# GpSimd gets xl and the scaling of r one attention slot later, from the seventh 128 tokens on

## The chip, the core and the metric

The kernel runs on one NeuronCore of a Trainium2 chip. TensorE (PE) multiplies matrices, VectorE (DVE), ScalarE (ACT) and GpSimd (POOL) work on tiles, and SyncE (SP) issues all DMAs here. Each engine runs its own instructions strictly in order. The metric is the time of one execution on the device in microseconds (us), the median of several runs.

## The reference

```python
def _attn_ref(r, k, v, w, u):            # (4, 8, 768, 48) each, u (8, 48)
    state = zeros((B, H, D, D))
    for t in range(S):
        cur = einsum('bhd,bhe->bhde', u[None] * kt, vt)
        y[:, :, t] = einsum('bhd,bhde->bhe', rt, state + cur)
        state = wt[:, :, :, None] * state + einsum('bhd,bhe->bhde', kt, vt)

x = y as (3072, 384)
h = x @ w_in;  g = h if h >= 1, 0 if h <= -1, else (h + 1)**2 / 4;  x = g @ w_out     # d_ff 2048
h = x @ w_in2; g = h * sigmoid(1.702 * h);                          out = g @ w_out2   # d_ff 2048
```

A linear attention with a decaying state (RWKV), then two MLPs on its 3072 tokens.

## The kernel before

**The MLPs.** Tokens are cut into eight tiles of 384, the hidden dimension into 16 pieces of 128. One step of the program (`step(s)`) is one piece of one tile: nine matmuls `gemm1` (`hp<-xh,whi`, `hp<-xl,whi`, `hp<-xh,wlo`), the activation, and nine matmuls `gemm2` (`acc<-...`) for the step three before (`LAG = 3`). Each float32 operand is split in a high and a low half to be multiplied in a faster format, so each product is three matmuls: `xh` and `xl` are the halves of the MLP's input, `gh` and `gl` those of the activation, `whi` and `wlo` those of the weights. In the first MLP the activation goes round the engines: VectorE clamps `hp` into `t` (L696), ScalarE squares it (L697), VectorE takes the maximum with `hp` (L709), ScalarE rounds that into `gh` (L690), and `gl = t - gh` (L684) goes to GpSimd in every second step and to VectorE in the others.

**The attention.** It is done in 24 windows of 128 tokens (`window(n)`, n from 0 to 23), six for each batch; three windows make the input of one MLP tile. While the MLP works on tile i, the windows of tile i+1 are woven in. `window` is a Python generator: each `yield` ends an attention slot, and `attn_slot` advances all open windows by one slot, the older first. A tile of 16 steps has 24 slots, so steps have one or two; a new window is opened when the one before has had eight. What a window does, by its slots:

- slot 1: VectorE's scans of the decay w (`pi<-rk`, L433 and L435) give the products `rr` and `pp`; GpSimd forms r*k*u (`rkn`, L436 and L437).
- slot 2: VectorE scales k with `rr` (L441), GpSimd scales r with `pp` (`rk<-rk,pi`, L443, called the scaling of r below).
- slot 3: ScalarE squares `pi` in place for a range check (L456), so after the scaling has read it; VectorE reduces `rkn` to `bb` (L457).
- slot 4: GpSimd's two selects put `bb` on the diagonal of `ra` (`ra<-bb`, L461); ScalarE copies the scaled r into the other half of `ra` (L469).
- slot 6: TensorE transposes k (`tp`, L476) and forms the scores (`sc`, L481); ScalarE copies `tp` to `ktok` (L483); VectorE merges the scores into `ra` under a mask (`ra<-mask,sc`, L486, called the merge below); GpSimd puts the carried state into `lt` (L452).
- slots 8 to 10: TensorE makes the state's update (`kv`, L505) and the output (`yt<-ra,lt`, L511); ScalarE copies it out (`xr`, L530), and six small DMAs move rows of it (L533).
- slot 12: ScalarE rounds `xr` into `xh` (L544), and `xl = xr - xh` (L545) follows, on VectorE for windows 0 to 5 and on GpSimd from window 6 on (`XL_N = 6`).

So slot 12 of window n-1 and slot 4 of window n are the same call, the older window first.

**The order.** The first 16 steps and the attention ahead of them are placed by a scheduler that works with a model of time. All later steps stand under `tc.manual_schedule()`: there each engine's order is the order in which the Python code issues the instructions. Beside this, weights of both MLPs are converted: for the second MLP VectorE takes the bits apart (L648, L650) and GpSimd adds the parts (`wt<-wt,wb`, L204), after which SyncE stores them.

Of the kernel before, what the change touches and what calls it, by code (L numbers as in the profile page):

```python
# [14 lines left out]
ALU = mybir.AluOpType  # L15
# [7 lines left out]
W = 128  # L23
# [38 lines left out]
XL_N = 6  # L62
# [37 lines left out]
def fast_path(st, tc, rkw_t, nat, v_l, w1, w2, u, out, x2_d, w2_d, flag_i, force):  # L100
    nc = tc.nc
# [248 lines left out]
    with ExitStack() as sa:  # L350
# [65 lines left out]
        def window(n):  # L416
            i = n % 2
            b, j = divmod(n, WPB)
# [9 lines left out]
            pp, rr = pi[:, 0:WW], pi[:, WW:2 * WW + 1]  # L428
# [11 lines left out]
            kw = rk[i][:, NP * W:OW].rearrange("p (a b) -> p a b", b=W)  # L440
            nc.vector.tensor_tensor(out=kw, in0=kw, in1=rr[:, 1:].rearrange("p (a b) -> p a b", b=W + 1)[:, :, 1:W + 1], op=ALU.mult)  # L441
            rw = rk[i][:, 0:NP * W].rearrange("p (a b) -> p a b", b=W)
            nc.gpsimd.tensor_tensor(out=rw, in0=rw, in1=pp.rearrange("p (a b) -> p a b", b=W + 1)[:, :, 0:W], op=ALU.mult)  # L443

            def lt_s(hh, c):
                p = slice(64 * hh, 64 * hh + D)
# [5 lines left out]
                    nc.gpsimd.tensor_tensor(out=lt_s(hh, 0), in0=us[p], in1=pcs[p, :, None].to_broadcast([D, NP, D]), op=ALU.mult)  # L452

            yield
            sq = pi.rearrange("p (a b) -> p a b", b=WW + 1)[:, :, 0:WW]
            nc.scalar.activation(out=sq, in_=sq, func=AF.Square, scale=DSC, accum_out=stat[:, n, 0:1])  # L456
            nc.vector.tensor_reduce(bb, nt[:, 0:MC * D].rearrange("p (a d) -> p a d", d=D), axis=AX.X, op=ALU.add)  # L457
            yield
            for hh in range(2):
                p = slice(64 * (1 - hh), 64 * (1 - hh) + 64)  # L460
# [6 lines left out]
            for hh in range(2):  # L467
                p = slice(64 * hh, 64 * hh + 64)
# [9 lines left out]
            for mc in range(MC):  # L478
                for hh in range(2):
                    p = slice(64 * hh, 64 * hh + D)  # L480
# [3 lines left out]
            for hh in range(2):  # L484
                p = slice(64 * (1 - hh), 64 * (1 - hh) + 64)
# [56 lines left out]
                xl[0, ti] = p2.tile([128, KD, TN], F32R, tag="xl", name="xl")  # L542
            o = xh[0, ti][:, :, off:off + W]
            nc.scalar.activation(out=o, in_=xr[:, 0:KD, :], func=AF.Copy)  # L544
            (nc.vector if n < XL_N else nc.gpsimd).tensor_tensor(out=xl[0, ti][:, :, off:off + W], in0=xr[:, 0:KD, :], in1=o.bitcast(F32), op=ALU.subtract)  # L545
            yield

# [7 lines left out]
        def attn_slot():  # L555
            n = started[0]
            if n < (NW if cur[0] >= 0 else MAXW) and n in vn_t and n in nat_t and (not queue or queue[-1][1] >= GAP[0]):
                started[0] += 1
                queue.append([window(n), 0, n, None])
            for e in list(queue):  # L560
                if e[3] == "x" and tile_of[e[2]][0] > cur[0] + 1:
                    continue
                try:
                    e[3] = next(e[0])
                    e[1] += 1
                except StopIteration:
                    queue.remove(e)
# [17 lines left out]
        with ExitStack():  # L585
# [6 lines left out]
            for hh in range(2):  # L592
                p = slice(64 * (1 - hh), 64 * (1 - hh) + 64)
# [280 lines left out]
```

## Time and profile before

| what | value |
|---|---|
| median of 3 runs | 1015.32 us (1013.87 to 1016.21) |
| the profiled execution's own time | 1015.02 us |
| its span, first to last instruction | 1013.3 us |
| mean granted TensorE clock | 0.975 of full speed |
| busy: TensorE, VectorE, ScalarE, GpSimd | 952.9, 567.3, 538.9, 400.0 us |

A busy TensorE is the rule in this kernel; the places that matter are those at which it waits, and what it waits for there. A row of the timeline gives in brackets the idle time of the engine just ahead of the instruction and what ended it.

### The profile page before, as it was taken

To read this page: it belongs to the slowest core of one execution; us is meant where nothing else is said; L and a number is where in the kernel's file an instruction comes from. 1 tells how busy PE (TensorE), PEld (TensorE's weight loads), DVE (VectorE), ACT (ScalarE), POOL (GpSimd) and SP (SyncE) were. 2 spreads that over 40 slices of the span, in tenths; PEclk is the share of its full clock that TensorE was granted. 3 is DMA by queue.
4 is the path that set the end of the run, shared out by engine and by line. 5 is a ranking of instruction groups with operands and counts; after the bars stand their busy time and mean duration, and the time that the engine had idled before them with its cause. 6 is when DMAs were issued, how large, how long until landed. Compare 5 with 4: busy or idle time off the path is not lost.

```text
span 1013.3 us, 18673 instructions
## 1 busy us (share of the span) xinstructions
PE 952.9 (94%) x6976; PEld 911.2 (90%) x6976; DVE 567.3 (56%) x983; ACT 538.9 (53%) x1279; POOL 400.0 (39%) x416
## 2 busy tenths in 40 slices
PE   4756999999999999999999999999999999999997
PEld 2545889899899899998999999999999999999997
DVE  6889966776777777677764753323232323232321
ACT  4666545666666567666554565555555433333332
POOL 5787744545556454565431441111111111111111
PEclk9957999999999999999999999999999999999999
DMA  8886515444545435553303352222222100000000
GB/s 233 206 227 170 138 25 161 131 116 134 151 125 138 138 99 137 137 153 99 92 20 109 105 155 86 86 87 86 86 86 86 41 22 26 22 24 25 24 1 27
DMA packets 52228, 101.73 MB, mean 100 GB/s; under 512 B 8608, under 2 KB 31392, under 8 KB 52128
## 3 DMA queue, kind: packets, MB, share of 16 engines
q1 hardware_dynamic: 52128, 100.45, 34.9%
q8 instruction: 57, 0.93, 0.4%
q14 instruction: 43, 0.35, 0.1%
HBM read 83.51 MB, written 15.73 MB: 98 GB/s over the span
## 4 chain that ended last, share of the span: by engine, by line
PE 62%; DVE 12%; ACT 9%; DMA 8%; issue 5%; SPq 4%; POOL 0%; ACTq 0%; DVEq 0%; POOLq 0%
PE hp L659 29%; PE acc L677 20%; PE acc L668 10%; DMA rk<-rkw_t 4%; SPq L533 3%; DMA xr<-xr 2%; DVE pi L433 2%; ACT gh L690 2%; DVE t L709 2%; DVE ra L486 2%; DVE pi L435 1%; ACT ra L469 1%; PE yt L511 1%; ACT t L697 1%; DMA wst<-w 1%
## 5 line engine op out<-in xcount | busy, mean ns | idle before, releaser
L684 POOL TENSOR_TENSOR gl<-t,gh 128x384 fp32r<-128x384 f32 x128 | 134.1, 1048 | 441.7 <-ACT gh L690 433.5
L690 ACT ACTIVATE gh<-t 128x384 fp32r<-128x384 f32 x256 | 133.9, 523 | 182.2 <-DVE t L709 77.7
L720 DVE TENSOR_TENSOR t<-t,hp 128x384 f32<-128x384 f32 x128 | 70.8, 553 | 218.6 <-ACT t L715 218.2
L715 ACT ACTIVATE t<-hp 128x384 f32<-128x384 f32 x128 | 62.9, 491 | 145.9 <-PE hp L659 145.8
L668 PE MATMUL acc<-gh,whi 128*128 128x384 f32 x384 | 132.8, 353 | 0.9 <-ACT ev L263 0.6
L668 PE MATMUL acc<-gl,whi 128*128 128x384 f32 x384 | 131.3, 342 | 2.3 <-DVE gl L684 2.3
L668 PE MATMUL acc<-gh,wlo 128*128 128x384 f32 x384 | 130.3, 339 | 0.0
L677 PE MATMUL acc<-wlo,gh 128*128 128x384 f32 x384 | 130.2, 339 | 0.0
L677 PE MATMUL acc<-whi,gh 128*128 128x384 f32 x384 | 129.9, 338 | 0.0
L677 PE MATMUL acc<-whi,gl 128*128 128x384 f32 x384 | 129.4, 337 | 0.0
L684 DVE TENSOR_TENSOR gl<-t,gh 128x384 fp32r<-128x384 f32 x128 | 78.3, 612 | 57.9 <-ACT gh L690 56.0
L697 ACT ACTIVATE t<-t 128x384 f32<-128x384 f32 x128 | 66.4, 519 | 68.5 <-DVE t L696 64.9
L709 DVE TENSOR_TENSOR t<-t,hp 128x384 f32<-128x384 f32 x128 | 70.1, 548 | 54.3 <-ACT t L697 52.8
L659 PE MATMUL hp<-xh,whi 128*128 128x384 f32 x384 | 92.0, 348 | 3.4 <-DVE t L709 3.3
L659 PE MATMUL hp<-xl,whi 128*128 128x384 f32 x384 | 89.4, 341 | 5.0 <-DVE xl L545 5.0
L696 DVE TENSOR_SCALAR t<-hp 128x384 f32<-128x384 f32 x128 | 70.4, 550 | 39.6 <-PE hp L659 39.4
L659 PE MATMUL hp<-xh,wlo 128*128 128x384 f32 x384 | 89.1, 341 | 0.0
L659 PE MATMUL hp<-x2l,whi 128*128 128x384 f32 x384 | 88.8, 339 | 0.0
L659 PE MATMUL hp<-x2h,wlo 128*128 128x384 f32 x384 | 88.0, 337 | 0.0
L659 PE MATMUL hp<-x2h,whi 128*128 128x384 f32 x384 | 87.4, 335 | 0.0
L668 PEld LDWEIGHTS acc<-gh,whi 128*128 128x128 f32 x384 | 72.4, 190 | 6.3 <-ACT ev L263 1.9
L668 PEld LDWEIGHTS acc<-gl,whi 128*128 128x128 f32 x384 | 72.9, 190 | 2.8 <-DVE gl L684 2.4
(107 smaller groups left out, 1865.4 us busy)
## 6 DMA issues: line engine op xcount, KB each, us to landing
wst<-w SPq DMA_DIRECT2D x96, 384.0 KB, 3.4
rk<-rkw_t SPq DMA_DIRECT2D x48, 288.9 KB, 4.9
rkn<-nat SPq DMA_DIRECT2D x24, 384.0 KB, 4.5
lt<-v_l SPq DMA_DIRECT2D x48, 128.0 KB, 3.8
w_d<-wt SPq DMA_DIRECT2D x32, 192.0 KB, 2.7
w2f<-w_d SPq DMA_DIRECT2D x32, 192.0 KB, 2.6
vn<-nat SPq DMA_DIRECT2D x24, 192.0 KB, 3.6
x_d<-ev SPq DMA_DIRECT2D x24, 192.0 KB, 2.2
```

The source lines that it names most:

```text
L433: nc.vector.tensor_tensor_scan(out=rr[:, WW:0:-1], data0=ws[:, WW:0:-1], data1=one_s[:, WW:0:-1], initial=0.0, op0=ALU.mult, op1=ALU.max)
L533: nc.sync.dma_start(out=xr[64 * hh + D:64 * hh + 64, q, :], in_=xr[64 * hh + 16 * q:64 * hh + 16 * q + 16, 3, :])
L659: nc.tensor.matmul(out=hp[:, 0:n], lhsT=win(a, f, kk), rhs=b[:, kk, 0:n], start=(i == 0), stop=(i == 3 * KD - 1))
L668: nc.tensor.matmul(out=acc[j][:, 0:n], lhsT=wout(a, f, j * 128, 128), rhs=b[:, 0:n], start=(f == 0 and i == 0), stop=(f == KF - 1 and i == 2))
L677: nc.tensor.matmul(out=o[:, 0:DM], lhsT=a[:, j * 128:(j + 1) * 128], rhs=wout(b, f, 0, DM), start=(f == 0 and i == 0), stop=(f == KF - 1 a ...
L684: eng.tensor_tensor(out=gl[:, 0:n], in0=t[:, 0:n], in1=gh[:, 0:n].bitcast(F32), op=ALU.subtract)
L690: nc.scalar.activation(out=gh[:, 0:n], in_=t[:, 0:n], func=AF.Copy)
L696: nc.vector.tensor_scalar(t[:, 0:n], hp[:, 0:n], scalar1=-1.0, scalar2=1.0, op0=ALU.max, op1=ALU.min)
L697: nc.scalar.activation(out=t[:, 0:n], in_=t[:, 0:n], func=AF.Square, bias=0.5, scale=0.5)
L709: nc.vector.tensor_tensor(out=t[:, 0:n], in0=t[:, 0:n], in1=hp[:, 0:n], op=ALU.max)
L715: nc.scalar.activation(out=t[:, 0:n], in_=hp[:, 0:n], func=AF.Sigmoid, scale=1.702)
L720: nc.vector.tensor_tensor(out=t[:, 0:n], in0=t[:, 0:n], in1=hp[:, 0:n], op=ALU.mult)
```

## The change

Two instructions of GpSimd are issued later, for the windows from n = 6 on. The scaling of r moves from the end of slot 2 to the start of slot 3, ahead of ScalarE's square of `pi`, which must come behind it. `xl` moves from slot 12 to a slot 13 of its own. Since slot 13 of window n-1 falls in the same call as slot 5 of window n, the selects of window n (slot 4) are now issued ahead of `xl` of window n-1. Nothing is added or removed, and no other engine's order changes in the part that is ordered by hand.

```diff
             rw = rk[i][:, 0:NP * W].rearrange("p (a b) -> p a b", b=W)
-            nc.gpsimd.tensor_tensor(out=rw, in0=rw, in1=pp.rearrange("p (a b) -> p a b", b=W + 1)[:, :, 0:W], op=ALU.mult)
+            if n < XL_N:
+                nc.gpsimd.tensor_tensor(out=rw, in0=rw, in1=pp.rearrange("p (a b) -> p a b", b=W + 1)[:, :, 0:W], op=ALU.mult)
...
             yield
+            if n >= XL_N:
+                nc.gpsimd.tensor_tensor(out=rw, in0=rw, in1=pp.rearrange("p (a b) -> p a b", b=W + 1)[:, :, 0:W], op=ALU.mult)
             sq = pi.rearrange("p (a b) -> p a b", b=WW + 1)[:, :, 0:WW]
             nc.scalar.activation(out=sq, in_=sq, func=AF.Square, scale=DSC, accum_out=stat[:, n, 0:1])
...
             nc.scalar.activation(out=o, in_=xr[:, 0:KD, :], func=AF.Copy)
+            if n >= XL_N:
+                yield
             (nc.vector if n < XL_N else nc.gpsimd).tensor_tensor(out=xl[0, ti][:, :, off:off + W], in0=xr[:, 0:KD, :], in1=o.bitcast(F32), op=ALU.subtract)
             yield
```

Since 24 slots fall on 16 steps, the neighbours of the moved instructions differ from window to window, with a period of three. GpSimd's queue of three windows that follow one another shows all three kinds. (The line numbers behind the change are a few higher: L545 becomes L550, L443 becomes L457, L461 becomes L464, L452 becomes L453, L684 becomes L689. `ra_3644` and so on are the buffers of one window's `ra`; L204 is the add for a weight piece.)

The first kind, here window 14, before:

```order
L443 TENSOR_TENSOR rk_163<-rk_163,pi 128x512
L684 TENSOR_TENSOR gl<-t,gh 128x384
L545 TENSOR_TENSOR xl<-xr,xh 128x3x128
L461 AFFINE_SELECT ra_3644<-bb 64x512
L461 AFFINE_SELECT ra_3645<-bb 64x512
L204 TENSOR_TENSOR wt<-wt,wb 128x384
L452 TENSOR_TENSOR lt_165<-us,pcs 48x4x48 x2
L684 TENSOR_TENSOR gl<-t,gh 128x384
```

and of the change:

```order
L457 TENSOR_TENSOR rk_163<-rk_163,pi 128x512
L689 TENSOR_TENSOR gl<-t,gh 128x384
L464 AFFINE_SELECT ra_3644<-bb 64x512
L464 AFFINE_SELECT ra_3645<-bb 64x512
L204 TENSOR_TENSOR wt<-wt,wb 128x384
L550 TENSOR_TENSOR xl<-xr,xh 128x3x128
L453 TENSOR_TENSOR lt_165<-us,pcs 48x4x48 x2
L689 TENSOR_TENSOR gl<-t,gh 128x384
```

The two selects and the add of a weight piece, which stood behind `xl`, now stand ahead of it.

The second kind, here window 15, before:

```order
L443 TENSOR_TENSOR rk_164<-rk_164,pi 128x512
L204 TENSOR_TENSOR wt<-wt,wb 128x384
L545 TENSOR_TENSOR xl<-xr,xh 128x3x128
L461 AFFINE_SELECT ra_3934<-bb 64x512
L461 AFFINE_SELECT ra_3935<-bb 64x512
L684 TENSOR_TENSOR gl<-t,gh 128x384
L204 TENSOR_TENSOR wt<-wt,wb 128x384
L452 TENSOR_TENSOR lt_166<-us,pcs 48x4x48 x2
```

and of the change:

```order
L204 TENSOR_TENSOR wt<-wt,wb 128x384
L457 TENSOR_TENSOR rk_164<-rk_164,pi 128x512
L464 AFFINE_SELECT ra_3934<-bb 64x512
L464 AFFINE_SELECT ra_3935<-bb 64x512
L689 TENSOR_TENSOR gl<-t,gh 128x384
L550 TENSOR_TENSOR xl<-xr,xh 128x3x128
L204 TENSOR_TENSOR wt<-wt,wb 128x384
L453 TENSOR_TENSOR lt_166<-us,pcs 48x4x48 x2
```

Here the selects and a `gl` moved ahead of `xl`, and the first add moved ahead of the scaling of r.

The third kind, here window 13, before:

```order
L443 TENSOR_TENSOR rk_164<-rk_164,pi 128x512
L684 TENSOR_TENSOR gl<-t,gh 128x384
L545 TENSOR_TENSOR xl<-xr,xh 128x3x128
L461 AFFINE_SELECT ra_3377<-bb 64x512
L461 AFFINE_SELECT ra_3378<-bb 64x512
L684 TENSOR_TENSOR gl<-t,gh 128x384
```

and of the change:

```order
L689 TENSOR_TENSOR gl<-t,gh 128x384
L457 TENSOR_TENSOR rk_164<-rk_164,pi 128x512
L464 AFFINE_SELECT ra_3377<-bb 64x512
L464 AFFINE_SELECT ra_3378<-bb 64x512
L550 TENSOR_TENSOR xl<-xr,xh 128x3x128
L689 TENSOR_TENSOR gl<-t,gh 128x384
```

A `gl` now stands ahead of the scaling of r, and the selects stand ahead of `xl`.

## Rows read from the trace of the kernel before

**Rows 1.** The page, part 2: TensorE's busy tenths in 40 slices of the span.

```profile
PE   4756999999999999999999999999999999999997
```

**Rows 2.** Waits of TensorE from 160 to 545 us: total us, times, longest.

```profile
PE kv L505 <- DVE ra L486: 5.3, 5, 2.1
PE yt L511 <- DVE ra L486: 4.0, 4, 1.7
PE kv L505 <- ACT ktok L483: 0.7, 1, 0.7
PE acc L668 <- ACT ev L263: 0.6, 3, 0.2
```

**Rows 3.** Waits of GpSimd and of VectorE from 160 to 545 us.

```profile
POOL xl L545 <- ACT xh L544: 75.1, 17, 6.8
POOL rk L443 <- DVE pi L435: 44.0, 16, 5.2
...
DVE ra L486 <- POOL ra L461: 13.5, 5, 2.8
```

**Rows 4.** VectorE's timeline, window 10 (third kind): start us, us, instruction, [idle before].

```profile
232.07 1.52 DVE L486 COPY_PREDICATED ra<-mask,sc 64x512 f32<-64x512 int32 x2 [2.83 <-POOL ra L461]
```

**Rows 5.** Timeline at window 11 (first kind).

```profile
251.51 1.01 POOL L545 TENSOR_TENSOR xl<-xr,xh 128x384 fp32r<-128x384 f32 x1 [3.51 <-DVE t L696]
...
252.60 1.67 POOL L461 TENSOR_SCALAR_AFFINE_SELECT ra<-bb 64x512 f32<-64x512 f32 x2
...
253.19 0.56 DVE L684 TENSOR_TENSOR gl<-t,gh 128x384 fp32r<-128x384 f32 x1 [1.70 <-ACT gh L690]
...
254.13 1.34 DVE L648 TENSOR_SCALAR wt<-wst 128x384 int32<-128x384 int32 x1
254.24 1.01 POOL L204 TENSOR_TENSOR wt<-wt,wb 128x384 int32<-128x384 int32 x1
...
256.28 1.50 DVE L486 COPY_PREDICATED ra<-mask,sc 64x512 f32<-64x512 int32 x2
...
256.37 0.58 ACT L483 ACTIVATE ktok<-tp 128x512 f32<-128x512 f32 x1
...
258.04 0.56 PE L505 MATMUL kv<-vn,ktok 64*48 64x48 f32 x16 [1.08 <-DVE ra L486]
```

**Rows 6.** Timeline at window 15 (second kind).

```profile
336.02 0.35 DVE L648 TENSOR_SCALAR wt<-wst 128x384 int32<-128x384 int32 x1
...
339.14 1.00 POOL L545 TENSOR_TENSOR xl<-xr,xh 128x384 fp32r<-128x384 f32 x1 [4.69 <-ACT xh L544]
...
340.81 0.55 DVE L709 TENSOR_TENSOR t<-t,hp 128x384 f32<-128x384 f32 x1 [3.37 <-ACT t L697]
...
342.01 1.95 DVE L684 TENSOR_TENSOR gl<-t,gh 128x384 fp32r<-128x384 f32 x1 [0.18 <-ACT gh L690]
...
342.54 0.99 POOL L204 TENSOR_TENSOR wt<-wt,wb 128x384 int32<-128x384 int32 x1
...
343.50 1.39 POOL L452 TENSOR_TENSOR lt<-us,pcs 48x192 f32<-48x192 f32 x2
...
345.72 0.78 PE L511 MATMUL yt<-ra,lt 128*64 128x64 f32 x16 [1.51 <-DVE ra L486]
```

**Rows 7.** TensorE's timeline at windows 8 (first kind) and 21 (second kind).

```profile
191.06 1.16 PE L505 MATMUL kv<-vn,ktok 64*48 64x48 f32 x30 [2.11 <-DVE ra L486]
...
475.55 1.06 PE L505 MATMUL kv<-vn,ktok 64*48 64x48 f32 x32 [0.72 <-ACT ktok L483]
478.33 1.20 PE L511 MATMUL yt<-ra,lt 128*64 128x64 f32 x16 [1.72 <-DVE ra L486]
```

**Rows 8.** Stretches: us, busy by engine, granted TensorE clock, DMA share, GB/s.

```profile
191.00:196.00 5.00, 4.95 (x59) 4.80 (x60) 3.64 (x9) 3.12 (x9) 2.63 (x3) 0.66 0.49 145
343.00:350.00 7.00, 5.49 (x70) 5.12 (x69) 4.97 (x10) 3.78 (x11) 5.16 (x7) 1.00 0.47 165
475.00:483.00 8.00, 5.72 (x62) 5.46 (x63) 5.91 (x10) 4.27 (x13) 6.16 (x8) 0.79 0.15 51
```

## The prediction

> **What bounds the kernel now.** I read the page's slices first. TensorE's busy share [rows 1] is low in the first four slices, about 100 us, in which the attention is started and weights are converted, and is 9 tenths from there to the end. So outside the start the kernel is bound by TensorE, and time can be won there only where TensorE waits or where its clock is lowered. The attention ends soon after 520 us, so the change has to work between about 160 us, where the first `xl` on GpSimd stands, and there. The list of TensorE's waits of that part [rows 2] is short and complete: 10.6 us in 13 waits, of which 9.3 us in nine waits end with VectorE's merge of the scores into `ra` (L486). They come at two of the three kinds of windows: at `kv` in the first kind (windows 8, 11, 14, 17, 20: 2.11, 1.08 and, from the sum of 5.3, three of 0.7), at `yt` in the second (windows 15 and 21: 1.51 and 1.72; windows 12 and 18 share the remaining 0.8) [rows 2, 5 to 7]. The third kind has none. Two places have a lower clock: 0.66 over the 5 us after 191, 0.79 over the 8 us from 475 [rows 8]. A mean below 1 in a stretch is time at 1.2 instead of 2.4 GHz. The wait of 1.51 at window 15 left the clock at 1.00 [rows 8], so in these rows the clock fell behind 2.11 us, and behind 0.72 and 1.72 us in close order, and not behind 1.51.
>
> Then I asked why the merge is late, in the timelines of both kinds. The obvious link is not the one that costs. VectorE does sit idle for GpSimd's selects ahead of the merge, 13.5 us in five waits [rows 3], but these five are the windows of the third kind, as window 10 [rows 4], at which TensorE does not wait. In the other two kinds VectorE has no idle time ahead of the merge: it is busy, and it is slow. At window 11 its L648 takes 1.34 us beside GpSimd's add L204, against 0.35 elsewhere [rows 5, 6]. At window 15 its `gl` takes 1.95 us beside GpSimd's L204 and the work ahead of it, against 0.56 [rows 5, 6]. So GpSimd's burst behind `xl` falls on the VectorE instructions just ahead of the merge. The burst starts there because GpSimd stands waiting for `xh` with everything else behind it, 75.1 us in 17 waits [rows 3].
>
> **The change, part by part.** *The scaling of r.* GpSimd idles ahead of it in all 16 windows of this part, until the scan L435 has written `pp` [rows 3]. Its start is thus set by the scan and not by its place in the queue, and I cost the later place at nothing for the scaling itself. In the first kind nothing passes it. In the second kind an add L204 (0.99 us) goes ahead into that idle time. In the third a `gl` goes ahead; if its `gh` comes late, the scaling starts up to 1.0 us later. ScalarE's square of `pi` waits behind the scaling, and the next `gh` and `t` queue behind that. What hides it: in 160 to 545 us TensorE never waits for `gh`, `gl` or a free `hp` [rows 2], although VectorE's L709 stood idle 3.37 us for a late `t` at window 15 [rows 6]. So the chain from `hp` to `gl` may be over 3 us late without cost; beyond that each further microsecond would be one of TensorE's.
>
> *The selects ahead of `xl`.* They need `bb`, which is there early, so they and the L204 behind them run in what was GpSimd's idle time before `xl`. `xl` itself starts when `xh` is there, as before; it has its reader in the next tile. What remains behind `xl` is shorter: at window 11, `lt` alone instead of selects, L204 and `lt`.
>
> First kind, from rows 5. Without L204 beside it L648 would take 0.35, so the merge comes 0.99 us earlier. `ktok`, which `kv` needs too, ends at 256.95, 1.09 us ahead of `kv`, and TensorE is free 1.08 ahead, so both allow it. Upper end: 0.99 at windows 8 and 11 and all 0.7 at the other three, 4.1 us. Against it: `xl` ends at 252.52 and `lt` (up to 1.39 us [rows 6]) then runs to 253.91 at most, right where VectorE's `gl` starts at 253.19. If that is held for 0.72 us, the merge and `ktok` are late by it, and 0.3 is left at each: 1.5 us. I take 2.8, the middle, since the rows put `lt` on the start of `gl` but do not say which is first.
>
> Second kind, from rows 6. `xl` 339.14 to 340.14, L204 to 341.13, `lt` to 342.52 at most, while `gl` is ready at 342.01. It is held for 0.51 at most instead of 1.39 (1.95 less 0.56). So the merge comes 0.9 to 1.39 earlier, at windows 15 and 21: 1.8 to 2.8 us, I take 2.4. Windows 12 and 18 I leave as they are.
>
> A rule of the Trainium skill bears on this: "SBUF — State Buffer", section "Who interferes with whom", says that a VectorE instruction with two inputs in SBUF contends with a GpSimd instruction that reads SBUF, and that the later one is blocked in full until the other is done. By it alone `gl` at window 15 would have waited for one GpSimd instruction; the trace shows it behind two in a row, through L204's end at 343.53 [rows 6], so I take the rows. The rule also speaks against the change, which puts the selects beside VectorE's L648 and L650 of the earlier steps; that is the third rival.
>
> *The clock.* 5 us at 0.66 lose 5 x 0.34 = 1.7 us, 8 us at 0.79 lose 8 x 0.21 = 1.7 [rows 8]. With the terms above the wait at window 8 shrinks from 2.11 to about 1.5 and that of window 21 from 1.72 to about 0.5. Both are then no longer than the 1.51 that left the clock alone, so I count both back: 3.4 us, with 0 as the other end.
>
> *The start.* Window 7's scaling leaves the part that the scheduler places, and a few neighbours swap there. TensorE's slices there are full already [rows 1]; I cost it at nothing, with 1 us to either side.
>
> Sum: 2.8 + 2.4 + 3.4 = 8.6 us off the profiled execution's 1015.0, which is 1006.4. The median of the runs stands 0.3 above that execution, so 1006.7 us. All upper ends (4.1 + 2.8 + 3.4 + 1) give 1004.0, all lower ends (1.5 + 1.8 + 0 - 1) 1013.0.
>
> **The rivals.** *The clock stays low.* The waits shrink as above but at one or both places the clock still falls. For it: the window 8 estimate of 1.5 us is at the edge. Gain 5.2 to 6.9, time 1008.4 to 1010.1, down to 1012 with the small ends of the first two terms.
>
> *Nothing changes.* The change removes what its form suggests, the waits for `xh` and for the selects, and these are idle time beside a busy TensorE: all of VectorE's 13.5 us lie at windows where TensorE doesn't wait. If VectorE's slow instructions are then hit by another GpSimd instruction (`lt`, or a `gl`) for as long, the merge stays where it is: 1015.3, give or take 1.5. Against it: less is left in GpSimd's queue behind `xl`.
>
> *The collisions move to a worse place.* The selects (1.67 us the pair) now run when VectorE works without a pause after the scans, and may stretch its L648 by 0.99 in each of 15 windows. VectorE's cover is the 3.37 us of idle time ahead of L709. It decides from the point at which the stretched chain is more than that late: then the merge is late in the first and second kinds, ten windows, by 1 us each, and with one more fall of the clock (1.7) the kernel ends at about 1015.3 + 10 - 5.2 + 1.7 = 1022 if nothing of the clock comes back; with half of the windows hit it is 1016.8, within the bound below. Against it: one collision of 0.99 is well inside 3.37.
>
> **How the numbers follow.** Chances: forecast 0.57 (own range 1004 to 1008.4), low clock 0.25, nothing 0.11, moved collisions 0.07. The range 1003.5 to 1012.5 takes in the first two with their bounds. Within 0.2%, about what a measurement of this kernel can tell from no change, is 1013.3 to 1017.3. So faster 0.82, same 0.11, slower 0.07.
>
> **What would show it.** In the profile after: GpSimd's wait ahead of `xl` remains but the selects stand ahead of it; VectorE's 13.5 us for selects are gone; L648 takes 0.35 and `gl` under 1.1 ahead of the merge at windows 11 and 15; TensorE's 9.3 us for the merge fall to about 4; the clock stays at 1.00 after 191 and 475. I am wrong if TensorE's waits for the merge are as long as before, if ScalarE waits for the scaling of r by more than a microsecond a window and TensorE for `gh` behind it, or if VectorE's time for L648 and L650 grows and L709 has no idle time left.

## The result and the profile after

The changed kernel takes 1003.62 us (median of 4 runs, 1002.71 to 1004.84). The kernel before, run beside it, took 1015.77 (4 runs, 1013.87 to 1018.0). The ratio is 0.989, 95% interval 0.9878 to 0.9902: 12.2 us faster by the medians (11.2 by the ratio), against 8.6 predicted. The profiled execution took 1002.71 us with a span of 1001.0, which is 12.3 less than before.

First TensorE's list of waits after the change, 160 to 545 us, which answers to [rows 2], and then rows of the same view for its weight loads, for ScalarE, VectorE and GpSimd (those three from 160 to 530 us). The columns are microseconds in total, times, and the longest.

```profile
PE yt L514 <- DVE ra L489: 1.4, 4, 0.4
PE kv L508 <- ACT ktok L486: 1.3, 2, 0.7
PE acc L673 <- ACT ev L263: 0.3, 1, 0.3
...
PEld acc L673 <- ACT ev L263: 2.3, 5, 0.6
...
ACT xh L547 <- DMA xr<-xr: 9.4, 10, 1.3
ACT pi L459 <- POOL rk L457: 3.9, 5, 0.8
...
DVE ra L489 <- PE sc L484: 1.6, 5, 0.3
...
POOL rk L457 <- DVE pi L435: 21.8, 11, 2.7
POOL xl L550 <- ACT xh L547: 19.7, 14, 2.4
...
POOL ra L464 <- DVE bb L460: 13.8, 5, 2.8
```

TensorE's 10.6 us are now 3.0, and none of `kv`'s waits ends with the merge any more. VectorE's 13.5 us for the selects [rows 3] are gone. Two waits are new that bear on the prediction: ScalarE's square of `pi` waits for the scaling of r, 3.9 us in five waits, and GpSimd's selects wait for `bb` at the five windows of the second kind, 13.8 us. These waits are from one execution. In a second profile of the same kernel (e11 below) TensorE's wait for `ktok` is 3.1 us instead of 1.3, and the other waits at `kv` and `yt` are within 0.2.

The timeline of windows 11 and 15 after the change, VectorE, GpSimd and the matmuls that waited, against [rows 5] and [rows 6]:

```profile
247.41 1.00 POOL L550 TENSOR_TENSOR xl<-xr,xh 128x384 fp32r<-128x384 f32 x1 [0.80 <-ACT xh L547]
248.37 1.08 POOL L453 TENSOR_TENSOR lt<-us,pcs 48x192 f32<-48x192 f32 x2
249.09 0.78 DVE L689 TENSOR_TENSOR gl<-t,gh 128x384 fp32r<-128x384 f32 x1 [1.43 <-ACT gh L695]
...
250.25 0.35 DVE L653 TENSOR_SCALAR wt<-wst 128x384 int32<-128x384 int32 x1
250.63 0.56 DVE L655 SCALAR_TENSOR_TENSOR wt<-wst,wt 128x384 int32<-128x384 int32 x1
...
251.23 1.52 DVE L489 COPY_PREDICATED ra<-mask,sc 64x512 f32<-64x512 int32 x2
...
253.38 0.56 PE L508 MATMUL kv<-vn,ktok 64*48 64x48 f32 x16
...
334.20 1.01 POOL L204 TENSOR_TENSOR wt<-wt,wb 128x384 int32<-128x384 int32 x1
...
335.17 1.08 POOL L453 TENSOR_TENSOR lt<-us,pcs 48x192 f32<-48x192 f32 x2
...
336.12 0.56 DVE L689 TENSOR_TENSOR gl<-t,gh 128x384 fp32r<-128x384 f32 x1 [0.18 <-ACT gh L695]
336.71 1.50 DVE L489 COPY_PREDICATED ra<-mask,sc 64x512 f32<-64x512 int32 x2
...
338.46 0.72 PE L514 MATMUL yt<-ra,lt 128*64 128x64 f32 x15
```

At window 11 L653 (the former L648) takes 0.35 instead of 1.34 us, `lt` stretches `gl` by 0.22, and `kv` starts without a wait. At window 15 `gl` takes 0.56 instead of 1.95, and `yt` starts without a wait. The stretches behind windows 8 and 21, where the clock was 0.66 and 0.79 [rows 8] (busy time and instructions of TensorE, its weight loads, VectorE, ScalarE and GpSimd; then the granted clock, the DMA share and GB/s):

```profile
189.00:194.00 5.00, 5.00 (x72) 4.63 (x74) 3.63 (x10) 3.35 (x9) 2.20 (x3) 1.00 0.51 146
466.00:474.00 8.00, 7.63 (x93) 7.10 (x94) 5.76 (x14) 4.73 (x13) 4.03 (x4) 1.00 0.30 72
```

Outside the windows little moved: window 7's `kv` starts at 166.6 us (167.3 before), and from window 23's `kv` to the end it takes 490.9 us (491.0). Between them it takes 343.5 us instead of 355.0, so 11.5 of the 12.3 lie there. Three parts make it up: the 7.6 us of waits (10.6 less 3.0), the two falls of the clock, which the prediction had priced at 3.4, and a wait that the prediction overlooked and that stands in the list of the weight loads before, not in that of the matmuls:

```profile
PEld acc L668 <- ACT ev L263: 1.9, 4, 0.6
...
PEld acc L668 <- DVE ev L261: 1.4, 4, 0.4
```

At the end of an MLP tile VectorE copies one accumulator out (`ev`, L261). In the third kind of windows this copy stood behind the late merge, and TensorE's next `acc` waited 0.35 us for it, four times. After the change that row is gone. With its 1.4 us the three make 12.4, which is 0.9 too much. Matching TensorE's matmuls of both timelines one by one gives less for two of them: 1.5 us at each fall of the clock, so 3.0, and 0.27 to 0.32 us at each of the four windows with `ev`, so 1.2 where the weight loads waited 1.4. The sum is then 11.8, against 11.5.

### The profile page after: what moved, and what is told of

Read it like the earlier page. It is cut to its first block, busy times and chain, and to the rows that moved or that the text cites. A ratio compares the mean times of both kernels' runs of the same rounds, so it can differ in the third digit from the quotient of the medians.

```text
span 1001.0 us, 18691 instructions
## 1 busy us (share of the span) xinstructions
PE 945.8 (94%) x6976; PEld 906.6 (91%) x6976; DVE 562.0 (56%) x983; ACT 538.2 (54%) x1279; POOL 393.4 (39%) x416
## 4 chain that ended last, share of the span: by engine, by line
PE 63%; DVE 13%; ACT 10%; DMA 5%; issue 5%; SPq 3%; POOL 0%; ACTq 0%; DVEq 0%
PE hp L664 29%; PE acc L682 20%; PE acc L673 10%; SPq L536 3%; DVE pi L433 2%; DMA rk<-rkw_t 2%; DMA xr<-xr 2%; ACT gh L695 2%; DVE t L714 2%; ACT ra L472 2%; DVE ra L489 2%; ACT t L702 2%; DVE pi L435 1%; PE kv L508 1%; PE yt L514 1%
## 5 line engine op out<-in xcount | busy, mean ns | idle before, releaser
L689 POOL TENSOR_TENSOR gl<-t,gh 128x384 fp32r<-128x384 f32 x128 | 132.5, 1035 | 497.0 <-ACT gh L695 465.5
L689 DVE TENSOR_TENSOR gl<-t,gh 128x384 fp32r<-128x384 f32 x128 | 75.4, 589 | 63.5 <-ACT gh L695 62.8
L714 DVE TENSOR_TENSOR t<-t,hp 128x384 f32<-128x384 f32 x128 | 70.2, 548 | 54.0 <-ACT t L702 52.5
```

Of the source, the lines that this page charges most:

```text
L689: eng.tensor_tensor(out=gl[:, 0:n], in0=t[:, 0:n], in1=gh[:, 0:n].bitcast(F32), op=ALU.subtract)
L714: nc.vector.tensor_tensor(out=t[:, 0:n], in0=t[:, 0:n], in1=hp[:, 0:n], op=ALU.max)
```

## Experiments

**Theory A:** what cost was GpSimd's burst behind `xl`, which fell on VectorE's last instructions ahead of the merge. With the selects ahead of `xl` it is shorter and earlier. **Rival B:** the later scaling of r carries the gain. **Rival C:** the selects came late for the merge. Each kernel was timed in five rounds; ratios are to the kernel before.

**e1, e2: the two halves of the change alone.** e1 has only this, e2 only the two other places of the diff:

```diff
             nc.scalar.activation(out=o, in_=xr[:, 0:KD, :], func=AF.Copy)
+            if n >= XL_N:
+                yield
             (nc.vector if n < XL_N else nc.gpsimd).tensor_tensor(out=xl...
```

> Only xl one slot later; the scaling of r stays where it was. Theory A (the burst of GpSimd's instructions that stood behind xl fell on VectorE's last instructions ahead of the merge; the selects, the adds L204 and gl now run ahead of xl, so the burst is shorter): nearly the whole gain of 12.2 us, 1003 to 1005.5 us, L648 at window 11 at 0.35 us and gl of VectorE at window 15 under 1.1 us. Rival B (the later scaling of r carries a good part): 1008 us or more. Rival C (what cost was that the selects came late for VectorE's merge): also the whole gain here.

> Only the scaling of r one slot later; xl and all behind it as before. Theory A: nothing of the burst behind xl changes, 1015.8 us, give or take 1.5, and TensorE's waits for the merge stay at 9.3 us. Rival B: 1004 to 1010 us. Rival C: 1015.8 us as A.

e1: 1002.29 us, 0.987 (0.985 to 0.9891). e2: 1017.35 us, 1.0013 (1.0 to 1.0026). The whole gain is in the place of `xl`; B falls. The scaling's move, alone, is no gain and perhaps a small loss (its profile has a third fall of the clock, at window 15).

**e3, e5, e6: `xl` later for one kind of window at a time.** In e3 (whose label is a slip: it is the first kind) the remainder is 1, in e5 2, in e6 0:

```diff
+            if n >= XL_N and n % 3 == 1:
+                yield
             (nc.vector if n < XL_N else nc.gpsimd).tensor_tensor(out=xl...
```

> xl one slot later only where the window that is then at slot 4 or 5 is of the first kind (8, 11, 14, 17, 20); the scaling of r as before. Theory A: the waits for the merge at kv (5.3 us) go and the clock behind window 8 comes back (1.5 to 1.7 us), the waits at yt (4.0 us) stay: 1008 to 1010.5 us. Rival C: VectorE's waits for the selects are at windows of the third kind, which this leaves as they were, 13.5 us in all: 1014 to 1016 us.

> xl one slot later only where the window then at slot 4 or 5 is of the second kind (9, 12, 15, 18, 21); the scaling of r as before. Theory A (shorter burst behind xl): the 4.0 us of waits at yt fall to about 0.7, the clock behind 476 comes back (1.5 us), the 5.3 us at kv and the clock behind window 8 stay: 1015 - 3.3 - 1.5 = 1010.2 us, 1009 to 1012. Rival C (late selects cost): VectorE's 13.5 us of waits for them are at the third kind, which stays: 1014 to 1016 us.

> xl one slot later only where the window then at slot 4 or 5 is of the third kind (10, 13, 16, 19, 22), where VectorE's merge waited 13.5 us for the selects; the scaling of r as before. Theory A: the 13.5 us go and TensorE hardly notices; from the shifts between the two first traces about 1.2 us in all: 1013 to 1015.5 us. Rival C: most of the gain is here, 1009 us or less.

First kind: 1009.63 us, 0.9946 (0.9927 to 0.9965), 5.5 us off. Second: 1009.45 us, 0.9934 (0.9921 to 0.9947), 6.7 off. Third: 1013.4 us, 0.9971 (0.9961 to 0.9981), 2.9 off. C, by which nearly all should lie in the third kind, falls as the main cause; but the third kind is worth more than the 0 of the prediction. The weight loads' waits show why. Those of e3, then of e6:

```profile
PEld acc L670 <- ACT ev L263: 1.3, 3, 0.5
PEld acc L670 <- DVE ev L261: 1.3, 4, 0.4
```

```profile
PEld acc L670 <- ACT ev L263: 1.3, 3, 0.5
```

The wait for `ev` stays where the third kind is as before, and goes in e6. The three gains add to 15.1 us. What they compare with is e1, which moves `xl` alone, with 13.2; the difference is within the intervals. Some may be counted twice: e6's profile also halves the waits at `kv` of windows 14, 17 and 20 (about 0.70 to 0.36, 0.44 and 0.39), which e3 wins too; and e5's has no fall of the clock behind window 8, although its wait there stayed at 2.01 us.

**e4: is it the add L204?** The kernel before, with L204 issued ahead of the first slot of its step, so ahead of `xl` in the first kind:

```diff
+            if l == 0 and i >= 1:
+                add_w2()
             if slots:
...
-                add_w2()
                 if f in PRE_F and nconv[1] < NPC:
```

> The kernel before, with GpSimd's add L204 issued ahead of the first attention slot of its step instead of behind it: in the first kind it then stands ahead of xl, while xl, the selects and the scaling of r stay as before; in the second kind the L204 behind xl keeps its place. Theory A, in the form that it is L204 that held L648: L648 at 0.35 us at windows 8, 11, 14, 17 and 20, most of the 5.3 us of waits at kv gone and the clock behind window 8 back: 1009 to 1012 us, with the 4.0 us at yt left. In the form that any instruction of GpSimd in that place costs the same: lt takes the place of L204, half of that gain, 1012 to 1014 us. Rival C (late selects): the selects are no earlier, 1015.8 us, give or take 1.5.

1011.52 us, 0.9963 (0.9948 to 0.9979). Its timeline at window 11 and, in the last two rows, at window 9 (here L649 and L651 are the former L648 and L650):

```profile
251.89 1.66 POOL L462 TENSOR_SCALAR_AFFINE_SELECT ra<-bb 64x512 f32<-64x512 f32 x2
252.47 0.56 DVE L685 TENSOR_TENSOR gl<-t,gh 128x384 fp32r<-128x384 f32 x1 [1.28 <-ACT gh L691]
...
253.41 0.36 DVE L649 TENSOR_SCALAR wt<-wst 128x384 int32<-128x384 int32 x1
253.52 1.39 POOL L453 TENSOR_TENSOR lt<-us,pcs 48x192 f32<-48x192 f32 x2
253.81 0.74 DVE L651 SCALAR_TENSOR_TENSOR wt<-wst,wt 128x384 int32<-128x384 int32 x1
...
256.77 0.43 PE L506 MATMUL kv<-vn,ktok 64*48 64x48 f32 x10
...
208.83 1.94 DVE L685 TENSOR_TENSOR gl<-t,gh 128x384 fp32r<-128x384 f32 x1 [0.18 <-ACT gh L691]
212.53 0.85 PE L512 MATMUL yt<-ra,lt 128*64 128x64 f32 x16 [1.73 <-DVE ra L487]
```

`xl` and the selects stand where they stood, `lt` has taken L204's place, and L649 takes 0.36: it was L204 that held it, and `kv` no longer waits. All of TensorE's waits for the merge at `kv` are gone from the list (2.4 us for `ktok` are left there); those at `yt` rose from 4.0 to 5.7 us. The rise is at window 9: 0.08 us of wait before, 1.73 here, with a fall of the clock behind it (1.41 in e3, with a fall too). VectorE's `gl` ahead of that merge takes 1.94 us, as in the kernel before (1.96), where TensorE came late enough not to wait for it. So part of the first kind's gain is given back one window later unless the second kind is mended too.

**e7: only the selects moved**, from slot 4 to the end of slot 3; `xl` and the scaling of r keep their slots, so L204 stays behind `xl`. The loop is cut from its place for n from 6 on:

```diff
             nc.vector.tensor_reduce(bb, nt[:, 0:MC * D]...
+            if n >= XL_N:
+                for hh in range(2):
+                    p = slice(64 * (1 - hh), 64 * (1 - hh) + 64)
+                    nc.gpsimd.affine_select(out=ra[hh][p]...
             yield
```

> The kernel before, with only the two selects issued one slot earlier, so that they stand ahead of xl; L204 of the first kind stays behind xl, and xl and the scaling of r keep their slots. Theory A: what stands behind xl is shorter by the selects in all kinds, so L204 runs beside gl or earlier instead of beside L648 and is over before the merge: 1004 to 1008 us. If it is L204's place behind xl as such that costs, whenever it runs: 1013 to 1015 us.

1003.44 us, 0.9877 (0.9862 to 0.9893): the gain of the whole change without moving either of its two instructions. Its timeline at window 11:

```profile
249.27 1.00 POOL L550 TENSOR_TENSOR xl<-xr,xh 128x384 fp32r<-128x384 f32 x1 [1.43 <-ACT xh L549]
250.23 1.01 POOL L204 TENSOR_TENSOR wt<-wt,wb 128x384 int32<-128x384 int32 x1
250.95 0.71 DVE L689 TENSOR_TENSOR gl<-t,gh 128x384 fp32r<-128x384 f32 x1 [1.73 <-ACT gh L695]
251.21 1.55 POOL L452 TENSOR_TENSOR lt<-us,pcs 48x192 f32<-48x192 f32 x2
...
252.05 0.35 DVE L653 TENSOR_SCALAR wt<-wst 128x384 int32<-128x384 int32 x1
```

Without the selects ahead of it L204 is nearly over when `gl` comes, and costs it 0.15 us.

**e8: the changed kernel with the selects behind `xl` again** (the same lines, at the start of slot 5):

```diff
                 nc.scalar.activation(out=ra[hh][p], in_=rt[p], func=AF.Copy)
             yield
+            if n >= XL_N:
+                for hh in range(2):
+                    p = slice(64 * (1 - hh), 64 * (1 - hh) + 64)
+                    nc.gpsimd.affine_select(out=ra[hh][p]...
             if n + 1 < NW:
```

> The changed kernel with the selects one slot later too, so behind xl again as before; in the first kind L204 stands ahead of xl, in the second and third kind the order behind xl is xl, selects, then L204 or gl. Theory A: first kind as with the add issued ahead (its waits at kv mostly gone), second kind as before (waits at yt 4 to 5.5 us, one or two falls of the clock): 1009.5 to 1012 us. If any instruction of GpSimd at that place cost VectorE as much, or the late selects themselves: 1014 to 1016 us.

1008.64 us, 0.993 (0.9917 to 0.9943), a little under the range: some 4 us (by the ratios) to 5 us (by the medians) of the gain are lost with the selects' place alone. VectorE's 13.5 us for them are back as 12.5, the wait for `ev` as 1.7, and at window 15:

```profile
337.63 1.02 POOL L204 TENSOR_TENSOR wt<-wt,wb 128x384 int32<-128x384 int32 x1
338.08 0.99 DVE L694 TENSOR_TENSOR gl<-t,gh 128x384 fp32r<-128x384 f32 x1 [0.19 <-ACT gh L700]
338.61 1.40 POOL L453 TENSOR_TENSOR lt<-us,pcs 48x192 f32<-48x192 f32 x2
```

GpSimd's `gl` has gone ahead of `xl` here, VectorE's `gl` is held by L204 alone, and takes 0.99 instead of 1.95.

**e9 to e12: is there more?** e9 is the changed kernel with `xh` in the later slot too. e10 is e7 with e1's edit as well. e11 is the changed kernel again. e12 is the kernel before with e9's edit, so with the scaling of r in its old slot:

```diff
             o = xh[0, ti][:, :, off:off + W]
+            if n >= XL_N:
+                yield
             nc.scalar.activation(out=o, in_=xr[:, 0:KD, :], func=AF.Copy)
-            if n >= XL_N:
-                yield
             (nc.vector if n < XL_N else nc.gpsimd).tensor_tensor(out=xl...
```

> The changed kernel with ScalarE's xh one slot later too, so that ScalarE does the copies of ra ahead of it and no longer holds them for the DMAs of xr (9.4 us in ten waits in the changed kernel). Theory A: what is left of TensorE's waits in the changed kernel is 1.3 us at kv for ktok, which stands late in ScalarE's queue, and 1.4 us at yt; the first goes, the second stays: 1001.5 to 1003 us against 1003.6. If xh and with it xl come so late that lt behind xl runs beside the merge's last predecessors again: 1005 us or more.

> The selects one slot earlier and xl one slot later, the scaling of r as before: both ways to get the selects ahead of xl at once. Theory A: each alone takes the same waits away, so both together give no more than one: 1002 to 1004 us. If the two gained by different waits, the gains add: below 1000 us.

> The changed kernel itself, for a comparison on the same chip with the two others: 1003.6 us, give or take 1. If the later scaling of r costs something (the kernel with only xl later had 1002.3 us): about 1 us above the others.

> xh and xl one slot later, the scaling of r in its slot of the kernel before. If the later scaling costs a little (the changed kernel lay 1 to 2 us above the two with the scaling as before): 998.5 to 1000 us. Theory A without that: the scaling does nothing either way, 1000.3 us, give or take 1.

e9: 1000.27 us, 0.9852 (0.9838 to 0.9866). e10: 1002.52 us, 0.9875 (0.9859 to 0.9891). e11: 1004.18 us, 0.9895 (0.988 to 0.991). e12: 998.28 us, 0.9829 (0.9813 to 0.9845), the fastest. e10 gives no more than e7, so the two ways win the same waits. Waits of TensorE and, as the third row, of ScalarE in e9; then TensorE's whole list in e12:

```profile
PE yt L514 <- DVE ra L489: 2.2, 5, 0.5
PE kv L508 <- ACT ktok L486: 1.3, 3, 0.8
...
ACT pi L459 <- POOL rk L457: 3.8, 5, 0.8
```

```profile
PE yt L511 <- DVE ra L486: 0.6, 2, 0.3
```

With the scaling in its old slot ScalarE's wait for it is gone and TensorE's 3.5 us of waits are 0.6. The intervals of e9 and e12 just overlap, and those of e1 (0.985 to 0.9891), the changed kernel and e11 do so widely. So a loss of about 2 us by the later scaling between e9 and e12, and of 1.3 to 1.9 between e1 and the changed kernel, is likely and not settled.

## Why the prediction was right, step by step

The mechanism held, but by the medians the gain of 12.2 us was more than all upper ends together, 11.3 (4.1 + 2.8 + 3.4 + 1). The measured 1003.62 us lies outside the forecast's own range of 1004 to 1008.4, and within the stated range by 0.12 us only. That it is within is partly luck: the first kind's term was too small, the third kind's was at nothing, and the clock came back in full for a reason that did not hold.

- **The cause** (GpSimd's burst behind `xl`, not the wait for the selects itself): right. e4 shows L204 holding L648, and e7 and e8 show that the selects' place ahead of or behind `xl` decides how late the burst is. "They need `bb`, which is there early" was wrong at the second kind: there the selects now wait up to 2.8 us for `bb`, which still leaves them ahead of `xl`.
- **First kind, 2.8 us (1.5 to 4.1): too small.** TensorE's waits there fell from 5.3 to 0.7, by 4.6, more than the upper end of 4.1 (to 1.2 in e11, by 4.1). The step that was off is "If that is held for 0.72 us": `lt` stretched `gl` by 0.22 at window 11, and L650, which took 0.74 there before (the row below), takes 0.56 now. Window 8 gained 1.4, more than L648's 0.99; there ScalarE's wait for the DMAs of `xr` was also shorter (1.53 to 0.89 us), which nothing here isolates.

```profile
255.50 0.74 DVE L650 SCALAR_TENSOR_TENSOR wt<-wst,wt 128x384 int32<-128x384 int32 x1
```

- **Second kind, 2.4 us (1.8 to 2.8): right in sum.** `yt`'s waits fell from 4.0 to 1.4, by 2.6. At windows 15 and 21 1.51 and 1.36 went, 2.9 in all and so a little over the upper end; window 9 waits 0.3 more than before. Windows 9, 12, 18 and 21 have 0.36 each.
- **The clock, 3.4 us: about right (3.0 in TensorE's matmuls), the reason too simple.** Both stretches are at 1.00. But that the clock falls behind a longer wait and not behind a shorter one does not hold (last section): in e5 and e6 it stays at window 8 with the wait nearly as it was. So that both falls are gone may in part be chance.
- **Third kind, nothing: wrong, 1.2 to 1.4 us.** "TensorE does not wait" was read from the matmuls' list; the weight loads' list had the wait for `ev`. The ranking stands: the third kind is worth least (e6).
- **The scaling of r, at nothing: probably wrong.** e12 against e9 and e2 against the kernel before say 1 to 2 us lost, at the edge of their intervals. The square of `pi` does wait behind it, 3.9 us in five waits, 0.8 at most, so under the stated microsecond a window. The cover that the prediction took for full is likely not: `ktok` stands further back in ScalarE's queue, and `kv` of windows 9, 12 and 18 waits for it for 1.1 to 1.4 us in all in e2, e8, e9 and e11, while no profile with the scaling in its old slot has more than 0.6 there. The first profile of the changed kernel has none there either, so this link is argued and not shown.
- **The start, nothing within 1 us:** window 7's `kv` lies at 165.5 to 168.2 us in all the profiles, and at 165.5 and 166.6 in the two of the changed kernel; the 0.7 us here are within that.
- **The rivals.** The low clock did not come. Collisions did move: beside the selects, in the step ahead, L653 takes 0.63 and L655 0.88 us at five windows (0.35 and 0.56 elsewhere). But VectorE's L714 (the former L709) still stood idle 2.79 us ahead of window 15's merge, so the cover held.

The rule of "SBUF — State Buffer", section "Who interferes with whom", in the Trainium skill says that where a VectorE instruction with two inputs in SBUF contends with a GpSimd instruction that reads SBUF, the one that comes later is blocked until the other is done. These traces agree: VectorE's stretched `gl` ends 0.42 or 0.43 us behind the end of the GpSimd instruction beside it, behind L204 in the kernel before at window 15, in e7 and in e8, and behind `lt` in the changed kernel at window 11. The limit is told below: in e8 `gl` was held by one L204, in the kernel before by two instructions in a row.

## What to carry to other kernels

When an engine idles ahead of an instruction and has urgent and unurgent work queued behind it, look at where the whole burst lands once the wait ends: on other engines it may hit exactly what is late. Issue the work that is ready ahead of the waiting instruction; here moving two selects one slot was worth as much as the whole change. And read the weight loads' waits beside the matmuls': a copy-out that queues behind a late instruction showed only there.

## What was not expected

**The clock does not fall by the length of the wait alone.** Two stretches behind window 8, of e5 and of e6, and `kv`'s waits there:

```profile
188.00:193.00 5.00, 2.99 (x57) 2.58 (x56) 4.21 (x7) 3.62 (x11) 4.77 (x7) 1.00 0.50 157
193.00:198.00 5.00, 5.00 (x42) 4.68 (x41) 4.27 (x9) 3.11 (x10) 1.84 (x2) 1.00 0.67 153
...
191.11 0.39 PE L505 MATMUL kv<-vn,ktok 64*48 64x48 f32 x9 [2.01 <-DVE ra L486]
```

```profile
188.00:193.00 5.00, 2.85 (x57) 2.44 (x56) 3.96 (x7) 3.63 (x12) 4.77 (x7) 1.00 0.44 144
193.00:198.00 5.00, 5.00 (x41) 4.68 (x40) 4.53 (x9) 2.84 (x8) 1.58 (x2) 1.00 0.76 168
212.00:216.00 4.00, 2.49 (x21) 2.40 (x22) 3.56 (x8) 2.25 (x7) 2.24 (x4) 0.75 0.16 62
...
190.86 0.34 PE L505 MATMUL kv<-vn,ktok 64*48 64x48 f32 x6 [2.15 <-DVE ra L486]
213.51 0.30 PE L511 MATMUL yt<-ra,lt 128*64 128x64 f32 x2 [1.60 <-DVE ra L486]
```

Behind 2.01 and 2.15 us the clock stayed at 1.00 (2.4 GHz all through), while the kernel before lost it behind 2.11 [rows 7, 8]; e6 lost it behind 1.60 and e3 behind 1.41 at window 9. At window 21 the kernel before fell behind 0.72 and 1.72 us, and e4, with 0.68 and 1.73, did not. What decides is open; a fall costs 1.5 us in TensorE's matmuls and 1.7 by [rows 8], and none of e1, e5 and e7 to e12 has one between 160 and 560 us.

**Which GpSimd instruction follows matters.** L204 coming directly behind another instruction held VectorE again (L648 1.34, `gl` 1.95 us [rows 5, 6]); `lt` coming directly behind the selects or L204 did not (L649 0.36 in e4, `gl` 0.99 in e8), though both start as close behind. Why is not settled.
